# One store transfer for two token halves, and stores held back behind crossbar transposes, in a linear-attention and MLP kernel

## The chip, the cores and the metric

The kernel runs on one core of a Trainium2 chip. The metric is the device time of one execution in microseconds (us). Before the change it was 218.69 us (median of three runs, 217.29 to 221.75). The engines are PE (matrix products), ACT, DVE and POOL (elementwise work), and SP, which here only issues DMA transfers; in the traces below they go out one after another, in program order. "PEld" is PE's weight load.

## The reference

Attention with a decay per head, in blocks, then an MLP with a quick GELU on the result:

```python
# q, k, v: (4 batches, 8 heads, 768 tokens, 64), lam: (8,), float32
for each block of tokens:
    intra = (q_b k_b^T * Dmask) v_b            # Dmask[i, j] = lam ** (i - j) for i >= j
    inter = (q_b * lam ** (i + 1)) kv_state
    out[block] = intra + inter
    kv_state = lam ** block * kv_state + (k_b * lam ** (block - 1 - i))^T v_b
x = out, tokens x (heads * 64)                 # 3072 x 512
h = x @ w_in                                   # 512 -> 2048
result = (h * sigmoid(1.702 h)) @ w_out        # 2048 -> 512, float32, 3072 x 512
```

## The kernel before

The 3072 tokens are worked in six waves of 512. Waves 0 and 1 take two batches each and 256 tokens of each. In them a pair of neighbouring tokens is split over the two halves of the partitions: partition `j * 64 + m` of an output tile holds row `2 * m + j`. Waves 2 to 5 take all four batches and 128 tokens of each, and there a partition is a row.

From wave 2 on, a wave's attention part needs, for each of four head pairs `p`, a crossbar transpose (a DMA transfer) of the scaled k and q (`kqs` to `kq`), and at its end one of the attention output (`xs` to `xT`), from which the MLP starts:

```python
def p_cast(w, p):                     # DVE scales k and q, POOL casts v, then
    ...
    nc.sync.dma_start_transpose(out=kq_of[w, p]..., in_=kqs...)      # "T0" to "T3"
def p_out(w, p):                      # PE, then
    xs = work.tile([P, B, 2, D], bf16, tag="xs", bufs=2, name="xs")  # two buffers
    nc.scalar.copy(xs..., o)
    nc.sync.dma_start_transpose(out=xT(w)[:, p], in_=xs...)          # "xT0" to "xT3"
```

The outputs are stored by SP too:

```python
op = ctx.enter_context(tc.tile_pool(name="op", bufs=4))
NR = 26                               # ring in which all loads land
def store(w, g, o, cols=slice(0, d_model)):
    if w < 2:
        r0 = (2 * w + g // 2) * S + (g % 2) * P
        dst = out[r0 : r0 + P, cols].rearrange("(m j) d -> j m d", j=2)
        for j in range(2):
            nc.sync.dma_start(out=dst[j], in_=o[hd(j), :])   # hd(j): 64 partitions
    else:
        r0 = g * S + w * P
        nc.sync.dma_start(out=out[r0 : r0 + P, cols], in_=o)
```

The program order is built by hand. `put` appends MLP work for PE and moves a clock of about a microsecond a unit; `at(t, ...)` puts attention work, loads and transposes between it at clock `t`. Around wave 2's start (`e` is the clock after wave 1's first two output groups):

```python
for g in range(2):
    for j in range(NJ):
        put(1, mlp2, 1, g, j)          # wave 1, output groups 0 and 1; their stores follow
e = clock[0]
full(e - 5.4, e + 1.2, 2, 2.2, 1.8)    # wave 2: casts and T0..T3 from e - 5.4, scores from e + 1.2
load_spread(e - 1, 3, 1.4)             # wave 3: 12 loads of 256 KB, 1.4 apart
for fc in range(FFC):
    put(0.5, fc_whole, 1, fc, HB)      # wave 1, second half of its first MLP product
for g in range(2, G):
    for j in range(NJ):
        put(1, mlp2, 1, g, j)          # wave 1, groups 2 and 3
```

## Time and profile before

| | before |
|---|---|
| median | 218.69 us |
| profiled run, span | 220.2 us |
| PE busy | 95% |
| PE's waits at 71 to 89 us | 3.7 us for T0 and T1, 1.2 us for ACT behind xT0 |
| a half store, issue to landing | 2.4 to 4.5 us, median 3.0 |

The profile page of the kernel before: busy time by engine, then three rows of the 40 slices of the span (tenths of busy time; PEclk is the granted TensorE clock in tenths; DMA is the mean of the core's 16 DMA engines).

```profile
PE 209.7 (95%) x1769; PEld 108.9 (49%) x1769; DVE 107.6 (49%) x235; ACT 87.9 (40%) x178; POOL 33.8 (15%) x66
...
PE   7989899999999499899999999999999999999994
...
PEclk9999999999999969999999999999999999999999
DMA  4999999997898999999969899577975132200112
```

PE is full nearly everywhere. The one dent after the start is slice 13 (71.6 to 77.1 us), followed by a slice with less clock. Who PE waited for there, in the view of waits (total us, times, longest):

```profile
PE ps_s L413 <- DMA kq<-kqs: 3.7, 2, 1.9
...
PE ps_o L443 <- ACT xs L453: 1.2, 1, 1.2
```

And what SP did in that stretch, in the timeline of SP's DMA issues (start us, us, what, how many):

```profile
62.54 7.29 SPq L496 DMA_DIRECT2D out_dram<-o_sb  x8
69.94 1.40 SPq L404 DMA_TRANSPOSE kq<-kqs  x1
71.43 1.18 SPq L496 DMA_DIRECT2D out_dram<-o_sb  x2
72.71 3.53 SPq L404 DMA_TRANSPOSE kq<-kqs  x2
76.29 0.58 SPq L101 DMA_DIRECT2D ring<-in_k_dram  x1
76.96 1.17 SPq L496 DMA_DIRECT2D out_dram<-o_sb  x2
78.24 1.37 SPq L404 DMA_TRANSPOSE kq<-kqs  x1
79.71 3.08 SPq L101 DMA_DIRECT2D ring<-in_k_dram  x3
82.89 1.69 SPq L454 DMA_TRANSPOSE xT<-xs  x1
```

Eight half stores of wave 0 take SP 7.3 us, and T0 goes out only behind them. The busy time by stretch (us; busy time and number of instructions of PE, PEld, DVE, ACT and POOL; granted clock; DMA share; GB/s). The DMA share adds up the durations of the packets that start in the stretch, so it can pass 1:

```profile
71.00:83.00 12.00, 8.28 (x104) 6.18 (x102) 7.48 (x18) 4.44 (x12) 0.00 (x0) 0.86 1.02 179
83.00:95.00 12.00, 10.83 (x103) 6.27 (x100) 5.05 (x10) 3.29 (x7) 0.00 (x0) 1.00 1.17 207
95.00:116.00 21.00, 21.00 (x178) 10.51 (x176) 13.44 (x32) 11.31 (x19) 2.29 (x4) 1.00 1.00 200
```

The lower clock (0.86) is one piece of 3.41 us at half rate, from 78.6 us. The Trainium skill says in "TensorE: Matmul & The Clock Gate", section "Part 1: The HAM clock gate", that PE's clock drops to half after an idle window, and that this window is 3413 ns. This trace agrees on the length: the half-rate piece lasts 3.41 us. It follows PE's two waits, of 1.9 and 1.8 us, but with work between them, so that no window was idle as a whole.

### The profile page before, as it was taken

To read this page: it belongs to the slowest core of one execution; us is meant where nothing else is said; L and a number is where in the kernel's file an instruction comes from. 1 tells how busy PE (TensorE), PEld (TensorE's weight loads), DVE (VectorE), ACT (ScalarE), POOL (GpSimd) and SP (SyncE) were. 2 spreads that over 40 slices of the span, in tenths; PEclk is the share of its full clock that TensorE was granted. 3 is DMA by queue.
4 is the path that set the end of the run, shared out by engine and by line. 5 is a ranking of instruction groups with operands and counts; after the bars stand their busy time and mean duration, and the time that the engine had idled before them with its cause. 6 is when DMAs were issued, how large, how long until landed. Compare 5 with 4: busy or idle time off the path is not lost.

```text
span 220.2 us, 4480 instructions
## 1 busy us (share of the span) xinstructions
PE 209.7 (95%) x1769; PEld 108.9 (49%) x1769; DVE 107.6 (49%) x235; ACT 87.9 (40%) x178; POOL 33.8 (15%) x66
## 2 busy tenths in 40 slices
PE   7989899999999499899999999999999999999994
PEld 2554344457854376444454444554444544444443
DVE  6686466572769748172664193572392532100121
ACT  5666661146612244246631056621076520366000
POOL 7593000373004000004000053000040000000000
PEclk9999999999999969999999999999999999999999
DMA  4999999997898999999969899577975132200112
GB/s 137 282 283 294 373 373 366 313 282 181 178 221 178 158 197 208 194 241 213 234 122 191 223 198 212 125 158 189 229 155 95 27 95 76 95 0 0 48 51 95
DMA packets 96742, 40.15 MB, mean 182 GB/s; under 512 B 77137, under 2 KB 89681, under 8 KB 96721
## 3 DMA queue, kind: packets, MB, share of 16 engines
q1 hardware_dynamic: 96576, 39.86, 75.9%
q8 instruction: 14, 0.23, 0.4%
q14 instruction: 8, 0.06, 0.1%
q10 hardware_dynamic: 144, 0.00, 0.0%
HBM read 27.27 MB, written 6.29 MB: 152 GB/s over the span
## 4 chain that ended last, share of the span: by engine, by line
PE 81%; DMA 11%; SPq 5%; DVE 1%; issue 0%; ACT 0%; ACTq 0%
PE ps_out L506 35%; PE ps_h L475 35%; SPq L89 4%; DMA kq<-kqs 3%; DMA ring<-in_moe_w_in_dram 3%; DMA xT<-xs 2%; PE ps_o L450 2%; PE ps_s L413 2%; DMA ring<-in_k_dram 2%; PE ps_out L521 2%; PE ps_o L443 1%; PE ps_kv L428 1%; PE ps_t L287 1%; PE ps_s L309 1%; SPq L117 1%; PE ps_o L382 1%
## 5 line engine op out<-in xcount | busy, mean ns | idle before, releaser
L475 PE MATMUL ps_h<-xT,w_in 128*128 128x512 bf16 (+1 forms) x448 | 88.5, 354 | 0.6 <-DVE w_in L150 0.6
L481 ACT ACTIVATE g_sb<-ps_h 128x512 bf16<-128x512 f32 (+1 forms) x112 | 59.1, 537 | 64.5 <-PE ps_h L475 63.7
L506 PE MATMUL ps_out<-w_out,g_sb 128*128 128x512 bf16 x368 | 83.4, 379 | 0.0
L475 PEld LDWEIGHTS <-w_in 128*128 128x128 bf16 x448 | 43.7, 100 | 39.8 <-DVE w_in L150 1.1
L506 PEld LDWEIGHTS <-g_sb 128*128 128x128 bf16 x368 | 34.7, 98 | 39.3
L513 DVE COPY o_sb<-ps_out 128x512 f32<-128x512 f32 x19 | 13.1, 691 | 53.6 <-PE ps_out L506 53.5
L420 DVE SCALAR_TENSOR_TENSOR sm<-ps_s,inv_pow,mask 128x512 bf16<-128x512 f32 x32 | 22.6, 747 | 28.0 <-PE ps_s L413 28.0
L453 ACT CAST xs<-ps_o 128x512 bf16<-128x512 f32 x16 | 9.4, 586 | 24.7 <-PE ps_o L450 21.8
L270 POOL TENSOR_TENSOR kqs<-ring,kq_pow 128x256 bf16<-128x256 f32 x16 | 10.3, 664 | 27.6 <-DMA ring<-in_q_dram 26.7
L402 POOL CAST v_bd<-ring 128x512 bf16<-128x512 f32 x8 | 4.9, 647 | 58.2 <-DMA ring<-in_v_dram 58.2
L402 POOL CAST v_sb<-ring 128x512 bf16<-128x512 f32 x8 | 7.2, 935 | 40.6 <-DMA ring<-in_v_dram 40.6
L314 DVE TENSOR_TENSOR sm<-ps_s,mask 128x512 bf16<-128x512 f32 x16 | 11.0, 684 | 2.7 <-PE ps_s L309 2.5
L432 DVE SCALAR_TENSOR_TENSOR kv<-kv,blk,ps_kv 64x256 bf16<-64x256 bf16 x24 | 11.4, 475 | 0.2
L400 DVE TENSOR_SCALAR kqs<-ring,q_pow 128x256 bf16<-128x256 f32 x32 | 11.2, 391 | 0.0
L400 DVE TENSOR_SCALAR kqs<-ring,k_pow 128x256 bf16<-128x256 f32 x32 | 10.5, 370 | 0.2
L262 PE MATMUL ps_f<-zeros 128*128 128x512 bf16 x25 | 9.2, 506 | 1.3 <-DVE zeros L180 1.3
L413 PE MATMUL ps_s<-kq 64*128 64x128 bf16 x128 | 6.4, 219 | 3.7 <-DMA kq<-kqs 3.7
L150 DVE CAST w_out<-ring 128x512 bf16<-128x512 f32 x16 | 7.2, 456 | 4.2 <-DMA ring<-in_moe_w_out_dram 4.2
L386 ACT CAST xT<-ps_o 128x256 bf16<-128x256 f32 x16 | 5.9, 371 | 8.3 <-DVE kv_bd L344 4.8
L270 DVE TENSOR_TENSOR kqs<-ring,kq_pow 128x256 bf16<-128x256 f32 x16 | 7.4, 482 | 3.0 <-DMA ring<-in_k_dram 2.3
L297 DVE COPY kq<-ps_t 128x512 bf16<-128x512 bf16 x10 | 4.2, 423 | 8.7 <-PE ps_t L287 8.7
L413 PEld LDWEIGHTS <-kq 64*128 64x128 bf16 x128 | 3.6, 94 | 9.8 <-issue 5.5
(68 smaller groups left out, 120.8 us busy)
## 6 DMA issues: line engine op xcount, KB each, us to landing
ring<-in_k_dram SPq DMA_DIRECT2D x23, 256.0 KB, 4.6
ring<-in_q_dram SPq DMA_DIRECT2D x23, 256.0 KB, 4.2
ring<-in_v_dram SPq DMA_DIRECT2D x23, 256.0 KB, 4.6
ring<-in_moe_w_in_dram SPq DMA_DIRECT2D x16, 256.0 KB, 6.4
ring<-in_moe_w_out_dram SPq DMA_DIRECT2D x16, 256.0 KB, 5.3
out_dram<-o_sb SPq DMA_DIRECT2D x15, 256.0 KB, 2.3
out_dram<-o_sb SPq DMA_DIRECT2D x16, 128.0 KB, 3.0
ring<-in_k_dram SPq DMA_DIRECT2D x2, 128.0 KB, 3.9
```

The lines of the kernel that those rows point to most:

```text
L270: eng.tensor_tensor(kqs_of[w, p][:, bl, i].rearrange("s j h d -> s h j d"), read(w, "kq"[i], bl, p), tab, op=MUL)
L314: nc.vector.tensor_tensor(sm.rearrange("s h j t -> s h (j t)"), s_ps.pop((w, bl, p))[:, :, 0 : 2 * P], mask2.to_broadcast([P, 2, 2 * P]), ...
L400: nc.vector.tensor_scalar(kqs[:, i, :, h, :], x[:, :, p, h, :], scalar1=(k_pow, q_pow)[i][:, 2 * p + h : 2 * p + h + 1], scalar2=None, op0 ...
L402: nc.gpsimd.tensor_copy(v_sb[w % 2][:, p], read(w, "v")[:, :, p])
L413: nc.tensor.matmul(s[:, h, b, :], t[hd(h), 0, b, :], t[hd(h), 1, b, :], start=True, stop=True)
L420: nc.vector.scalar_tensor_tensor(sm[:, h], s[:, h], inv_pow[:, 2 * p + h : 2 * p + h + 1], mask.to_broadcast([P, B, P]), op0=MUL, op1=MUL)
L432: nc.vector.scalar_tensor_tensor(new[hd(h), p], old[hd(h), p], blk2[hd(h), p : p + 1], t[hd(h), :, hd(h)], op0=MUL, op1=ADD)
L453: nc.scalar.copy(xs.rearrange("s b h d -> s h b d"), o)
L475: nc.tensor.matmul(t[:, bs[0] * P : bs[1] * P], w_in_sb[fc // CW][:, kc, (fc % CW) * P : (fc % CW + 1) * P], xT(w)[:, kc, bs[0] : bs[1], : ...
L481: nc.scalar.activation(g_tile(w)[:, fc, c], h_ps.pop((w, fc))[:, c], GELU)
L506: nc.tensor.matmul(t, g_of[w][:, fc, g * P : (g + 1) * P], w_out_sb[j][:, fc % CW, :], start=(fc == 0), stop=(fc == FFC - 1))
L513: nc.vector.tensor_copy(o, t)
```

## The change

Its intent: half as many store instructions on SP, and wave 0's stores out of the way of wave 2's transposes. Two more output buffers hold them back; the ring gives up two of 26 slots for the room.

```diff
-    op = ctx.enter_context(tc.tile_pool(name="op", bufs=4))
+    op = ctx.enter_context(tc.tile_pool(name="op", bufs=6))
-    NR = 26
+    NR = 24
@@ store @@
-            dst = out[r0 : r0 + P, cols].rearrange("(m j) d -> j m d", j=2)
-            for j in range(2):
-                nc.sync.dma_start(out=dst[j], in_=o[hd(j), :])
+            nc.sync.dma_start(out=out[r0 : r0 + P, cols].rearrange("(m j) d -> j m d", j=2),
+                              in_=o)
@@ mlp2 @@
-            store(w, g, o)
+            if w == 0:
+                kept.append((w, g, o))
+            else:
+                store(w, g, o)
+    kept = []
+    def store_kept():
+        store(*kept.pop(0))
@@ schedule of wave 2 @@
-        full(e - 5.4, e + 1.2, 2, 2.2, 1.8)
+        full(e - 6.6, e + 1.4, 2, 2.2, 1.8)
+        for t in (-0.8, -0.8, 0.4, 0.4):
+            at(e + t, store_kept)
```

## The prediction

> **What bounds it now.** PE is busy 95% of 220.2 us (page, part 1) and PE lines make 81% of the chain that ended last. What is left to win here is small: in the waits of PE, 3.7 us on DMA kq<-kqs and 1.2 us on ACT xs (itself held by xT<-xs), all at 71 to 89 us. The timeline shows why: the SP queue spends 62.5 to 69.8 us issuing eight half stores of wave 0, so wave 2's first crossbar transpose issues only at 69.9, and two more half stores sit between it and the second. After that pause the granted clock is 0.62 at 79 to 83 us (busy time by stretch), worth about 1.5 us. So the intended gain is at most some 5 to 6 us.
>
> **Intent.** 16 half stores (about 0.58 us of SP issue each) become 8; those of wave 0 go behind the four transposes, which start about 2 us earlier. The ring of 24 should cost little.
>
> **What I expect instead.** The new destination's slowest dimension is j, of size 2 (the order of instructions shows 2x64x512); the source's is 128. The Trainium skill, "DMA: Bandwidth & Descriptors", section "Why a DMA increments its semaphore by 16 and not by 1", says a transfer is split over the largest k up to 16 that divides both slowest dimensions. Here k is 2. No transfer of the kernel before has such a shape, but all I read (64 or 128 rows) show sixteen separate completion increments in the trace, which agrees. So each merged store puts 64 packets of 2 KB on each of two DMA engines. An undisturbed late store shows 82 to 87 ns per such packet: 64 x 83 ns = 5.3 us on those two engines (estimate) instead of 0.7 us on sixteen.
>
> Everything behind needs its share on those two engines. Order on SP: T0, store, T1 to T3, a k load, five stores together, three k loads, xT0. Work on the slow pair from 69.5 us: store 5.3, three transposes about 0.8 each, load 1, five stores 26.5, three loads 3, xT0 0.5. So T1 lands near 77 (as before), and the first xT lands near 108 us instead of 88.3. With two xs buffers, ACT's third xs waits for it, and PE behind ACT at ps_o L443: a stall of about 20 us. Later the stores of wave 1's groups 2 and 3 (10.6 us) delay wave 3's first kq transpose to about 130 to 133 us, when PE would want it at about 124 to 126: some 4 to 7 us more. The gain at 71 us (about 2) is swallowed, as the later waits are absolute.
>
> Sum: 218.7 + 20 + 5.5, minus 1 = **243 us**, range 230 to 256. Chances: over 2% faster 0.08, within 2% 0.03, slower 0.89.
>
> **Signs.** Merged stores land in 6 us or more, in the group of five up to 25 to 30; of each one's increments fourteen come at once at issue. PE waits near 87 to 108 us for ACT xs L453, and that for DMA xT<-xs; a second wait for kq<-kqs of wave 3. DMA share drops to about two engines' worth (0.1 to 0.2) at 85 to 105 us. After about 135 us the stages keep their lengths.
>
> **What would make it wrong.** If the transfer runs on sixteen engines, stores land in 2 to 3 us, the waits at 71 to 89 us mostly vanish, and the time is 213 to 216. If packets on two engines go faster than 83 ns, the loss is smaller; if full queues block SP's issue as well, larger.

## The result, and the profile after

The changed kernel is correct and takes 255.05 us (median of four runs, 254.18 to 257.87), beside 219.18 us for the kernel before in four runs. The ratio is 1.169 (1.155 to 1.183). Here and below a ratio is the mean time of one kernel's fast runs over that of the other's of the same rounds, so not quite the ratio of the medians quoted. Executions over 1.5% slower than the fastest of the same kernel are left out of the means.

The same parts of the page, of the profiled run of the changed kernel (span 256.2 us):

```profile
PE 214.6 (84%) x1769; PEld 110.6 (43%) x1769; DVE 109.1 (43%) x235; ACT 87.9 (34%) x178; POOL 31.2 (12%) x66
...
PE   8889999999794920029916999999999999999995
...
PEclk9997999999997985557975999999999999999999
DMA  5999999999279111479499698897788713310022
```

Counted from 0, PE's row has dents at slice 12, at 14 to 17 (90 to 115 us) and at 20. The DMA row reads 1 at slices 13 to 15: about two of sixteen engines are busy. PE's waits, and under them ACT's wait behind the first:

```profile
PE ps_o L443 <- ACT xs L453: 22.3, 1, 22.3
PE ps_s L413 <- DMA kq<-kqs: 11.3, 2, 7.7
```
```profile
ACT xs L453 <- DMA xT<-xs: 26.2, 2, 24.8
```

ACT's copy in wave 2's third `p_out` needs an `xs` buffer, both are waiting for their transpose, and PE's next product needs the PSUM tile that this copy empties. xT0 landed at 112.98 us instead of 88.27. The timeline of SP shows what stood in front of it:

```profile
70.39 0.68 SPq L494 DMA_DIRECT2D out_dram<-o_sb  x1
71.61 8.80 SPq L404 DMA_TRANSPOSE kq<-kqs  x3
80.46 0.58 SPq L101 DMA_DIRECT2D ring<-in_k_dram  x1
81.14 14.93 SPq L494 DMA_DIRECT2D out_dram<-o_sb  x5
96.17 13.30 SPq L101 DMA_DIRECT2D ring<-in_k_dram  x3
109.57 1.62 SPq L454 DMA_TRANSPOSE xT<-xs  x1
```

Five stores and three loads hold SP for 28 us. The view of the store's line (ns: least, median, most) gives

```profile
L494 SPq DMA_DIRECT2D out_dram<-o_sb x8: 525/753/4946, 70.4 to 126.8; - x8
```

so a store's issue took 0.5 us when nothing held it and up to 4.9 us here. From 82.4 to 109.5 us SP stood at six issues in a row: three stores (3.7, 4.7 and 4.9 us) and three loads (4.9, 4.95 and 3.3 us). The stretches as before:

```profile
71.00:83.00 12.00, 8.33 (x85) 6.04 (x83) 7.77 (x21) 3.65 (x9) 0.00 (x0) 0.89 0.88 109
83.00:95.00 12.00, 8.45 (x99) 5.84 (x98) 5.41 (x10) 3.65 (x9) 0.00 (x0) 0.93 0.14 51
95.00:116.00 21.00, 2.28 (x20) 1.25 (x20) 0.00 (x0) 1.17 (x2) 0.00 (x0) 0.50 0.44 112
```

From 83 to 95 us the DMA engines are 0.14 busy, which is 2.2 of 16, and move 51 GB/s.

The trace also keeps every increment of each transfer's completion semaphore. Read out of the trace for the merged stores of the changed kernel (times in us, not a view of the profile):

```
store (wave, group)   issued   increments recorded          landed   after the one before
w1 g0                  70.39   3: at +1.06, +7.91, +7.95     78.34
w1 g1                  81.14   3: at +0.95, +8.03, +8.04     89.18
w0 (four, kept)        81.77   3: at +1.04, +12.50, +12.51   94.28    5.10
                       82.45   3                             99.40    5.12
                       86.29   3                            104.52    5.12
                       91.13   3: at +5.36, +18.51, +18.52  109.65    5.13
k load behind them     96.17   16                           110.55
xT0                   109.57   16                           112.98
w1 g2                 118.70   3                            126.77
w1 g3                 126.83   3                            135.19
T0 of wave 3          127.76   16                           136.93
```

Every transfer of the kernel before has sixteen increments. A merged store has one at issue and two at landing (the records give no amounts, so that the one at issue stands for fourteen, as the prediction says, is not shown), and stores in a row land 5.12 us apart: 64 packets in 5.12 us on each of two engines is 80 ns a packet. The DMA packets of the trace say the same: while w1 g0's store ran, 128 packets of 2 KB started, about 12 in each half microsecond once it was under way, median 84 ns each.

One trap: the page's group of store issues hides all this.

```profile
out_dram<-o_sb SPq DMA_DIRECT2D x23, 256.0 KB, 2.4
```

The median of 2.4 us to landing looks healthy. It comes from only three of the 23 stores in this group, all of them whole stores of the later waves: the view pairs increments with transfers by sixteens, so it gives no landing for a merged store, nor for any other transfer whose semaphore also served a merged one.

Where the 36 us came from, as the lengths of stages between the first gelus of waves and halves in the two profiled runs:

| stage, to the end of a first gelu | before | after | difference |
|---|---|---|---|
| start to wave 1's first half | 53.38 | 55.05 | +1.7 |
| wave 1's first half to its second | 17.20 | 18.75 | +1.6 |
| wave 1's second half to wave 2 | 25.74 | 48.38 | +22.6 |
| wave 2 to wave 3 | 31.88 | 41.95 | +10.1 |
| wave 3 to the last output copy | 89.34 | 89.34 | 0.0 |

The profiled run was the slowest of the changed kernel's four (the one before was the slowest of its own, too); the +1.7 of the start is not seen in any other run (the kernels below are 0.4 to 1.5 us ahead of the profiled kernel before at that point), so it is taken as scatter of that run.

### The profile page after: what moved, and what is told of

Same layout as the page of the kernel before. It is cut to its first block, busy times and chain, and to the rows that moved or that the text cites. A ratio compares the mean times of both kernels' runs of the same rounds, so it can differ in the third digit from the quotient of the medians.

```text
span 256.2 us, 4459 instructions
## 1 busy us (share of the span) xinstructions
PE 214.6 (84%) x1769; PEld 110.6 (43%) x1769; DVE 109.1 (43%) x235; ACT 87.9 (34%) x178; POOL 31.2 (12%) x66
## 4 chain that ended last, share of the span: by engine, by line
PE 69%; SPq 13%; DMA 12%; DVE 3%; issue 1%; ACT 0%; POOL 0%; DVEq 0%; ACTq 0%
PE ps_h L475 31%; PE ps_out L505 28%; DMA kq<-kqs 7%; SPq L101 6%; SPq L89 4%; SPq L494 3%; DMA ring<-in_moe_w_in_dram 2%; PE ps_o L450 2%; PE ps_s L413 2%; DMA ring<-in_v_dram 1%; PE ps_out L528 1%; DMA xT<-xs 1%; PE ps_kv L428 1%; PE ps_o L443 1%; DVE sm L314 1%
## 5 line engine op out<-in xcount | busy, mean ns | idle before, releaser
L475 PE MATMUL ps_h<-xT,w_in 128*128 128x512 bf16 (+1 forms) x448 | 90.3, 359 | 1.0 <-POOL w_in L150 0.9
L505 PE MATMUL ps_out<-w_out,g_sb 128*128 128x512 bf16 x368 | 85.0, 385 | 0.0
L443 PE MATMUL ps_o<-kv,kq 64*128 64x64 bf16 x128 | 4.8, 196 | 22.3 <-ACT xs L453 22.3
L443 PEld LDWEIGHTS <-kq 64*128 64x128 bf16 x128 | 3.5, 98 | 23.9 <-issue 23.9
L400 DVE TENSOR_SCALAR kqs<-ring,k_pow 128x256 bf16<-128x256 f32 x32 | 12.0, 415 | 0.2
L413 PEld LDWEIGHTS <-kq 64*128 64x128 bf16 x128 | 3.9, 98 | 17.4 <-DMA kq<-kqs 12.1
L402 POOL CAST v_sb<-ring 128x512 bf16<-128x512 f32 x8 | 4.9, 648 | 44.9 <-DMA ring<-in_v_dram 44.9
L262 PE MATMUL ps_f<-zeros 128*128 128x512 bf16 x25 | 8.6, 478 | 1.3 <-DVE zeros L180 1.3
```

What stands on the lines that cost most here:

```text
L400: nc.vector.tensor_scalar(kqs[:, i, :, h, :], x[:, :, p, h, :], scalar1=(k_pow, q_pow)[i][:, 2 * p + h : 2 * p + h + 1], scalar2=None, op0 ...
L413: nc.tensor.matmul(s[:, h, b, :], t[hd(h), 0, b, :], t[hd(h), 1, b, :], start=True, stop=True)
L443: nc.tensor.matmul(o[:, h, b, :], kq_of[w, p][hd(h), 1, b, :], kv_sb[w % 2][hd(h), p, b, :], start=(b == 0), stop=True, skip_group_check=True)
L475: nc.tensor.matmul(t[:, bs[0] * P : bs[1] * P], w_in_sb[fc // CW][:, kc, (fc % CW) * P : (fc % CW + 1) * P], xT(w)[:, kc, bs[0] : bs[1], : ...
L505: nc.tensor.matmul(t, g_of[w][:, fc, g * P : (g + 1) * P], w_out_sb[j][:, fc % CW, :], start=(fc == 0), stop=(fc == FFC - 1))
```

## The experiments

The theory: the merged store's destination has a leading dimension of 2, so the transfer runs on two DMA engines, and what is behind it waits. Rivals: the new place of the stores (in front of wave 2's xT), merging as such, rows that do not follow one another, the ring of 24. Twelve runs of eleven kernels were made, on four chips; ratios are to the kernel before in the same rounds.

| run | what | median us | ratio | correct |
|---|---|---|---|---|
| changed kernel | leading dimension 2, kept back | 255.05 | 1.169 | yes |
| halves_kept | halves, kept back | 223.44 | 1.019 | yes |
| merged_only | leading dimension 2, old places | 250.29 | 1.141 | yes |
| rows4 | leading dimension 4, kept back | 240.28 | 1.099 | no |
| rows16 | leading dimension 16, kept back | 220.65 | 1.007 | no |
| natural | 128 consecutive rows, kept back | 219.26 | 0.998 | yes |
| natural_unkept | 128 consecutive rows, old places | 219.02 | 0.998 | yes |
| ring24 | ring of 24 alone | 219.60 | 1.004 | yes |
| late | natural, stores behind each xT | 219.65 | 1.002 | yes |
| pool_queue | changed kernel, stores from POOL | 240.40 | 1.108 | yes |
| natural_spread | natural, later loads | 217.76 | 1.002 | yes |
| natural_spread_again | the same once more | 217.78 | 0.995 | yes |
| spread_casts | natural_spread, casts as before | 218.72 | 1.007 | yes |

By the record's verdicts the changed kernel and merged_only are slower; halves_kept, rows4, pool_queue, spread_casts and the first natural_spread are "unclear" at the 2% mark, though the intervals of rows4 (1.092 to 1.105) and pool_queue (1.093 to 1.122) lie far above 1; the others are the same.

### The store alone undone: halves_kept

```diff
-            nc.sync.dma_start(out=out[...].rearrange("(m j) d -> j m d", j=2), in_=o)
+            dst = out[r0 : r0 + P, cols].rearrange("(m j) d -> j m d", j=2)
+            for j in range(2):
+                nc.sync.dma_start(out=dst[j], in_=o[hd(j), :])
```

> The changed kernel with only its store undone: two transfers of 64 partitions each again, still kept back behind the four transposes, ring of 24. If the leading dimension of 2 (two DMA engines) is the cause, every half store lands in 2 to 4 us, PE's 22.3 us wait at ps_o goes, and the time is 215 to 221 us. If instead the new place of the stores, in front of wave 2's xT transposes, is the cause (bytes and place are the same here), the wait at ps_o stays at 10 us or more and the time is over 235 us.

Measured: 223.44 us (222.52 to 224.25), ratio 1.019 (1.013 to 1.026). The half stores land in 2.3 to 3.6 us. PE's largest wait is now

```profile
PE ps_o L443 <- ACT xs L453: 5.6, 1, 5.6
```

So the shape of the store is worth about 32 of the 36 us. But the time is above what I expected: with everything kept back as intended and no slow store, the kernel is still slower than before. Ten half issues (75.1 to 82.3 us on SP) now stand in front of xT0. The rival of the place is right about that much.

### The merged store at the old places: merged_only

```diff
 # the kernel before, with only
-            for j in range(2):
-                nc.sync.dma_start(out=dst[j], in_=o[hd(j), :])
+            nc.sync.dma_start(out=out[...].rearrange("(m j) d -> j m d", j=2), in_=o)
```

> The kernel before with only its store changed: the merged store with leading dimension 2, at the old places, nothing kept back, ring of 26. Two-engine theory: six merged stores of 5.1 us each stand in front of or between wave 2's transposes instead of behind them, so PE waits early, for kq<-kqs (over 15 us in all near 70 to 95 us), and again for wave 3; 243 to 257 us. Place theory: nothing was kept back, so about 219 us.

Measured: 250.29 us (249.03 to 250.95), ratio 1.141. The wait is where the stores now stand, in front of T0 to T3:

```profile
PE ps_s L413 <- DMA kq<-kqs: 23.9, 3, 14.6
PE ps_o L443 <- ACT xs L453: 3.0, 1, 3.0
```

Keeping the stores back is not what costs the 36 us, nor does it avoid them.

### One transfer, scattered rows, sixteen groups: rows16

```diff
-    out[...].rearrange("(m j) d -> j m d", j=2)
+    out[...].rearrange("(m j) d -> j m d", j=16)
```

The result is wrong (rows land permuted within a tile).

> The changed kernel, but the destination is split in 16 groups of 8 rows instead of 2 of 64 (a wrong result on purpose: rows of a tile land permuted). Still one transfer from 128 partitions, still rows that do not follow one another, same bytes, same place. Leading-dimension theory: 16 divides 128, sixteen engines, sixteen completion increments, stores land in 2 to 4 us, 215 to 221 us. If merging as such or scattered rows is the cause: stores land in over 6 us and the time stays over 240 us.

Measured: 220.65 us (219.53 to 221.72), ratio 1.007 (0.999 to 1.014). Each store has sixteen increments and lands in 2.9 to 4.6 us. It is still one merged transfer with a stride between rows, at the same place with the same bytes. So neither merging nor scattered rows is the cause; the leading dimension is.

### Four groups: rows4

```diff
+    out[...].rearrange("(m j) d -> j m d", j=4)
```

> The changed kernel with the destination split in 4 groups of 32 rows (wrong rows on purpose). Leading-dimension theory: four engines, 32 packets of 2 KB each, so stores in a row land 2.6 us apart (5.1 us in the changed kernel); the first xT lands some 15 us earlier than its 113.0 us, PE's wait at ps_o falls from 22.3 to 5 to 10 us and the wait for wave 3's kq to under 2 us; 225 to 234 us. If a store only has a fast kind (sixteen) and a slow one (anything strided in few groups), it stays at 250 us or more, or falls to 220.

Measured: 240.28 us (239.64 to 240.77). Each store has five increments in the trace, one at issue and four at landing, and three of the four steps between stores of the group are 2.57, 2.57 and 2.55 us, half of 5.12. That is the dose expected: the number of engines is the leading dimension. xT0 landed at 97.08 us, 15.9 earlier than in the changed kernel, as expected. But the time is above the 225 to 234 us that I wrote, and so are the waits:

```profile
PE ps_o L443 <- ACT xs L453: 12.3, 1, 12.3
PE ps_s L413 <- DMA kq<-kqs: 7.4, 2, 5.3
```

A store that is not in such a row was not twice as fast: the three of this kind took 6.4 to 7.8 us to land here and 7.9 to 8.4 with two engines. In the packet records such a store's first packet starts 1.3 to 2.3 us after its issue. In its first four half microseconds 6 to 13 packets start with two engines and 1 to 15 with four; later it is some 12 with two and up to 25 with four. Why is open. So the loss is not proportional to the packets per engine: it fell from 35.9 to 21.3 us where they were halved.

### The same intent with sixteen engines: natural

ACT's cast that writes the MLP's input of waves 0 and 1 puts the tokens into natural order. Output tiles then hold consecutive rows, and the transfer has a leading dimension of 128:

```diff
-        nc.scalar.copy(xT(w)[:, p, 2 * bl : 2 * bl + 2, :], uo_ps...[:, :, 0:P])
+        nc.scalar.copy(xT(w)[:, p, 2 * bl : 2 * bl + 2, :].rearrange("c x (m j) -> c x j m", j=2),
+                       uo_ps...[:, :, 0:P].rearrange("c x (j m) -> c x j m", j=2))
...
+            nc.sync.dma_start(out=out[r0 : r0 + P, cols], in_=o)
```

> The changed kernel made good: ACT writes xT of waves 0 and 1 with tokens in natural order (a strided write in 16 casts), so the output tile's partitions are consecutive rows and one transfer of 128x2048 bytes with leading dimension 128 stores it; result right. Two-engine theory: stores land in 2 to 3 us, half of the SP issues of the halves are saved, 213 to 219 us; the 16 casts take perhaps 0.1 us longer each. If merging is the cause: over 240 us.

Measured: 219.26 us (218.42 to 222.22), ratio 0.998 (0.989 to 1.007). The stores land in 2.0 to 4.1 us. The slow store is gone, but the time is just above the 213 to 219 us expected, and no gain is left either:

```profile
PE ps_o L444 <- ACT xs L454: 3.1, 1, 3.1
```

The trace shows a gain that is given back. At the end of wave 1's last gelu the run is 5.9 us ahead of the profiled kernel before (79.64 against 85.52 us); at wave 2's first gelu only 2.3. Between lie this wait, 3.1 us, and a half-rate piece of 3.41 us from 86.4 us, worth half of that; the kernel before waits 1.2 us there.

### Merging alone, done right: natural_unkept; the ring alone: ring24

```diff
 # natural_unkept: the kernel before, with the cast and the store of "natural", nothing else
 # ring24: the kernel before, with
-    NR = 26
+    NR = 24
```

> The kernel before with natural rows, so one merged store with leading dimension 128, at the old places, nothing kept back, ring of 26, casts as before. Fewer and shorter issues on SP (four of about 0.4 us instead of eight of about 0.6 us) let wave 2's first transpose issue about 2 us earlier than 69.9 us, so PE's waits for kq<-kqs (3.7 us) fall to about 1 us; 215.5 to 219 us. If keeping back is what frees the transposes, about 219 us.

> The kernel before with a ring of 24 instead of 26 and nothing else. If the ring's size is not what costs, the ratio is within 1% of 1. If it delays the loads of weights at the start, the first ps_h comes 1 us or more later and the ratio is over 1.01.

Measured: 219.02 us, ratio 0.998 (0.990 to 1.005), and 219.60 us, ratio 1.004 (0.998 to 1.009). A merged store on sixteen engines is worth nothing that can be measured at the old places, and the ring's size costs nothing that can be. The first is a small miss: I had hoped for a gain of up to 1.5%.

With the stores kept back it is otherwise. natural and halves_kept ran in the same rounds, both with kept stores; they differ in the shape of the store and the cast that goes with it. natural is 4.2 us shorter (219.26 against 223.44; ratios 0.989 to 1.007 against 1.013 to 1.026). Five issues (3.06 us of SP) stand in front of xT0 there, against ten (7.19 us). rows16, merged too but with the old cast, is 2.8 us shorter than halves_kept. So fewer store instructions did pay, where the stores stood in the way.

### Where should the kept stores stand: late

```diff
 # natural, with
-        for t in (-0.8, -0.8, 0.4, 0.4):
+        for t in (3.8, 6.0, 8.2, 10.4):        # one behind each xT
```

> The kernel with natural rows, but wave 0's four kept stores go one by one behind each of wave 2's xT transposes instead of in front of the first. In the run with natural rows PE was 5.9 us ahead of the kernel before at wave 1's mlp2 of group 2, and 3.1 us of that went back in the wait at ps_o for the first xT, with 3.4 us at half clock after it. If the kept stores in front of xT cause that wait, it falls to under 1 us and the time is 213 to 217 us. If the three k loads and wave 1's stores hold xT, little changes: 217 to 220 us.

Measured: 219.65 us (217.22 to 220.85), ratio 1.002 (0.996 to 1.008), a miss. The wait moved rather than went. It is now at wave 2's MLP, for the last xT, behind the stores and loads between the xTs:

```profile
PE ps_h L476 <- DMA xT<-xs: 2.1, 1, 2.1
```

This profile is of the slowest of its six runs, so only the place of the wait is read from it.

### Loads of wave 3 later: natural_spread, natural_spread_again, spread_casts

```diff
 # natural_spread: natural, with
-        load_spread(e - 1, 3, 1.4)
+        load_spread(e + 3, 3, 1.2)
 # spread_casts: natural_spread, with
-        full(e - 6.6, e + 1.4, 2, 2.2, 1.8)
-        for t in (-0.8, -0.8, 0.4, 0.4):
+        full(e - 5.4, e + 1.4, 2, 2.2, 1.8)
+        for t in (0.4, 0.4, 0.9, 0.9):
```

> The kernel with natural rows; wave 3's loads start 4 us later (one of them in front of the first xT instead of four) and follow one another 1.2 us apart. With natural rows PE was 5.9 us ahead of the kernel before and lost 3.6 us in the wait for the first xT and the half clock after it; with the kept stores moved behind xT it lost as much, later, in the wait for the fourth xT. If the queue in front of the xT transposes as a whole is what gives the gain back, the first xT lands 3 us earlier, the wait falls to under 1 us, and the time is 213 to 216.5 us. If wave 3's loads are then late, a new wait for kq<-kqs of wave 3 appears and the time is 217 to 221 us.

> As natural_spread, with wave 2's casts back where the kernel before had them (1.2 units later) and wave 0's stores about 1 unit later, still behind the fourth kq transpose. In all runs with the early casts the stage from wave 1's first gelu to its second half's first gelu took 17.6 to 19.1 us, in those without 17.2 us. If the casts stand in front of wave 1's own work on DVE, this stage is 17.2 us again and the time is 0.5 to 1.5 us below natural_spread; if they are needed early for the transposes, waits for kq<-kqs come back and it is not faster.

> The same kernel as natural_spread once more, to see whether its lead is real: its six runs were 217.3 to 218.9 us, all at a granted clock of 1.0, beside a kernel before that scattered from 215.8 to 220.9 us, so that the verdict by fast runs (1.002) and the medians (217.8 against 219.9 us) disagree. If the lead is real: a median 1 to 2.5 us below that of the kernel before, again with every run's clock at 1.0. If it was the scatter of the kernel before: medians within 0.5 us.

Measured: natural_spread 217.76 us (217.26 to 218.89) beside 219.94 for the kernel before, and again 217.78 (216.95 to 219.11) beside 219.69. xT0 landed at 81.10 us instead of 85.17 in "natural". PE's waits in the profiled run:

```profile
PE ps_s L414 <- DMA kq<-kqs: 1.4, 1, 1.4
...
PE ps_h L476 <- DMA xT<-xs: 1.0, 1, 1.0
```

In all twelve runs the granted clock is 0.999 or 1.0, while thirteen of the 22 runs of the kernel before beside them have 0.992, the half-rate piece. So what gave the gain back was the queue in front of xT0: with the stores moved (late) the wait came back at the last xT, with three of four loads moved it is gone, although the stores still stand there. That is the first outcome of the expectation, but the time is above its 213 to 216.5 us, and time and waits fit the second. The 1.4 us wait is for wave 3's first kq (it ends at 99.16 us; the repeat has the same wait), and the stage from wave 2's first gelu to wave 3's is 33.3 us in both profiled runs, where "natural" has 31.9: the later loads push wave 3's transposes back. How large the gain is stays uncertain. By medians it is 1.0% and 0.9%. By fast runs the ratios are 1.002 (0.995 to 1.009) and 0.995 (0.989 to 1.000); in the first set one run of the kernel before at 215.79 us made seven of its eleven runs count as slow. It is the fastest correct version by median.

spread_casts took 218.72 us (218.33 to 220.03), ratio 1.007. Its stage from wave 1's first half to its second is 17.19 us, as in all kernels with the old casts (17.19 to 17.20 in four others), against 17.6 to 19.1 in those with casts 1.2 units earlier: the early casts do stand in front of wave 1's own work on DVE. But PE's waits for kq<-kqs are 2.0 us in its profile, and it is not faster.

### The stores on another queue: pool_queue

```diff
 # the changed kernel, with
-            nc.sync.dma_start(out=out[...].rearrange("(m j) d -> j m d", j=2), in_=o)
+            nc.gpsimd.dma_start(out=out[...].rearrange("(m j) d -> j m d", j=2), in_=o)
```

> The changed kernel, merged stores with leading dimension 2 as they are, but issued from POOL's queue instead of SP's. If what costs is that SP's queue is in order and fills up behind the stores (SP stood 4.9 us at an issue five times), SP's transposes and loads now share the two engines with the stores packet by packet: PE's wait at ps_o falls from 22.3 us to under 8 us, and the time is 220 to 230 us, although each store still takes 5 us or more. If the two engines' occupation holds the rest whatever queue the stores are on, the wait stays over 15 us and the time over 240 us.

Measured: 240.40 us (239.64 to 241.88), ratio 1.108. (In the trace four issues of SP took 4.7 to 4.95 us, not five.) Neither outcome as written: the wait at ps_o fell as the first theory says, and the time stayed as the second does.

```profile
PE ps_s L413 <- DMA kq<-kqs: 13.7, 4, 4.6
PE ps_o L443 <- ACT xs L453: 2.9, 1, 2.9
```

Stores took 8.8 to 19.0 us to land and transposes beside them up to 16.4. But the run is not clean: POOL's stores have sixteen increments and 512 packets of 4 KB in all, and up to 105 of these started within 2 us, which is 215 GB/s and more than two engines moved above (51 GB/s). The other queue also changed how the transfer is cut. How much of the 36 us is due to SP's order, and how much to the two engines being busy, stays open.

## Why the prediction was right or wrong

**Right: the mechanism and the direction.** The prediction read the leading dimension of 2 and, from the Trainium skill ("DMA: Bandwidth & Descriptors", section "Why a DMA increments its semaphore by 16 and not by 1"), concluded that two engines carry the store. The runs agree in four doses: two groups, three increments and 5.12 us a store; four groups, five increments and 2.56 us; sixteen groups or 128 rows, sixteen increments and 2.0 to 4.6 us to landing. The 5.3 us a store was 5.12.

**Right: both waits and their order.** PE waited at ps_o for ACT and that for xT0, then for wave 3's T0; the DMA share fell to 0.14 there; from wave 3 on the stages are equal to 0.01 us. Whether what is behind a merged store waits for SP's order or for the two engines is not separated (pool_queue).

**Wrong: the size.** A loss of 24.3 us was forecast (243 against 218.7) and 36 measured, although 255.05 lies just inside the range. Three terms of the sum failed.

- "4 to 7 us more" for wave 3's transpose, taken as 5.5, was 10.1. T0 landed at 136.93 us where the prediction had 130 to 133. The two stores in front of it were priced at 10.6 us together, 5.3 each; neither stood in a row behind another, and they took 8.1 and 8.4 us to land, the second issued only when the first had landed. The wait itself was 7.7 us, and the half-rate clock after it cost about 2.5 (5.0 us of busy time at half rate, 136.9 to 141.9). The prediction priced the half clock for the old pause, and left it out for the two it forecast (4.3 us of PE's work after the first ran at half rate, too, from 113.7 to 118.0 us).
- "a stall of about 20 us" was a wait of 22.3 us in a stage that grew by 22.6. The prediction let the slow pair start at 69.5 us and T1 land "near 77 (as before)". The first store's packets began at 71.67 us and T1 landed at 80.89, a wait of 3.6 us. The group of five then ran 5.12 us apart as forecast, from a later start, and xT0 came 5 us later than the 108 forecast.
- "minus 1" was a plus of 3.2. Of this 1.6 us is the early casts in front of wave 1's work on DVE; spread_casts removes it. The other 1.7 us, at the start, is scatter of the profiled run as far as the runs show. The gain at 71 us never appeared: T0 did come early (71.11 instead of 73.10 us), but T1 came later.

**Wrong in detail: a single store's landing.** "In the group of five up to 25 to 30" us from issue was 18.5 at most, since SP could not issue the later ones at once: they stood 3.7 to 4.9 us at the issue. The prediction had named a blocked issue only as a way to be wrong.

**Wrong: what the intent is worth.** It said 213 to 216 us should sixteen engines carry the store. Four kernels where they do and the stores are kept back took 219 to 223 us (natural, late, rows16, halves_kept). The gain of 5.9 us is there at the end of wave 1's gelu in "natural", but most of it goes back in the wait for xT0 and the half clock after it, because the stores held back behind T0 to T3, and wave 3's first loads, stand in front of xT0. With the loads moved later and the stores left there (natural_spread) some 2 us stay by medians.

## What to carry to other kernels

Before merging two transfers, look at the outermost dimension of both access patterns: merging 64 partitions twice into `2 x 64` rows left two of sixteen engines, and everything behind in that queue inherited the delay, far from the line that was edited. Count the completion increments of a changed transfer in the trace rather than trust a median over a group. And a transfer moved out of the way of one consumer is moved into the way of the next: ask what stands behind its new place, and what a short idle of PE costs again in clock.

## What the Trainium skill lacked or had wrong

- "DMA: Bandwidth & Descriptors", "Rules for kernel authors", says of two transfers to disjoint partition halves: "Don't bother"; use one transfer of 128 partitions. Here merging made the whole kernel take 1.14 times as long (merged_only), since its DRAM side had a leading dimension of 2. The row "Use all 16 engines" of the same table gives the reason; the first row lacks the reference to it. Merged with 128 leading rows, the time equals that of the halves (0.998).
- The same page, section "Why a DMA increments its semaphore by 16 and not by 1", agrees with the runs on how k, the number of engines, is chosen (leading dimensions of 2, 4, 16 and 128). It has no time for a transfer on few engines: a store of 256 KB took 5.12 us for k = 2 and 2.56 for k = 4, in a row. The page's "Specifications" only give a bandwidth per engine.
- No page that I read says what a full queue does to the issuer: SP stood 4.7 to 4.95 us, four times, at an issue that otherwise takes about 0.55, with two to three earlier transfers outstanding, and loads and transposes behind were held before they were even issued.
- "TensorE: Matmul & The Clock Gate" speaks in Part 1 and in its rules of idle gaps of about 3 us and more, and under "A second HAM failure mode" of micro-idles, to which it gives no length. Here two gaps of 1.9 and 1.8 us with 2.5 us of work between them were followed by 3.41 us at half clock. In ring24's profiled run gaps of 0.7, 1.8 and 2.2 us, with 2.7 and 8.8 us of work between them, were not. The lengths of half-rate pieces (3.41, 6.83, 10.24, 23.89 us) are whole multiples of its 3413 ns window.
- No page that I read gives what a single store of k = 2 or 4 takes, one that does not stand in a row: it took 6.4 to 8.4 us to land where its packets account for 2.6 to 5.1. (On sixteen engines a late store took 1.9 us at best, with 0.7 for its packets.) The cause of the rest was not found.
